# Two casts of v set behind the first product's copy, and down projection rows evicted with high priority

## The chip, the cores and the metric

The kernel runs on one core of one Trainium2 chip. Its time is the device time of one launch in microseconds, as the median of several runs. Engines are named as in the profile: PE is TensorE (matmuls; PEld are its weight loads, which overlap them), DVE is VectorE, ACT is ScalarE, POOL is GpSimd and SP is SyncE. An "ACTq" or "SPq" in front of a line is the engine's own queue issuing a DMA.

## What is computed

Attention with a window of 128 keys and a linear bias per head, over 8 batches, 8 heads, 576 positions and 64 columns per head; its output, with the heads side by side, goes through a bilinear feed-forward layer (512 to 1536 to 512). Everything is float32 at the interface.

```python
scores = scale * np.matmul(q, k.transpose(0, 1, 3, 2))
scores = np.where(mask, scores + bias[None], -1000000000.0)
attn = np.exp(scores - np.max(scores, axis=-1, keepdims=True))
attn = attn / (np.sum(attn, axis=-1, keepdims=True) + 1e-09)
x = np.matmul(attn, v)          # heads laid side by side: 4608 x 512
out = (x @ w_a) * (x @ w_b) @ w_out
```

## The kernel before

The float32 operands are split into two float16 parts each (a rounded one and the rest), and every product is three float16 matmuls into PSUM: high by high, high by low, low by high. Scales that are powers of two keep the parts in range.

The work is woven from two streams. One is the feed-forward layer, batch after batch: an up projection (`up`) and a down projection (`down`). The other is the attention of the batches to come, in steps of one pair of heads (`attention`, four pairs to a batch). A `Pace` object lets the attention advance by a given share at each step of the projections, so that PE always has dense matmuls of the one beside the small ones of the other. During `down` of batch b the attention works through pairs 0 and 1 of the batch after next, and the step that comes with the first step of the next `up` is that for pair 2.

From batch 3 on (and for half of batch 2) the up projection is `up_fast`, a scheme with seven products in place of eight for each of twelve blocks of 128 hidden columns, in steps of six matmuls of 128 x 288. For one block: the first product goes into the PSUM bank `ch`, and ACT copies it to `x0` (line 801). The second goes into another bank, and DVE adds it to `x0` (line 807). The third is *added into* `ch` (so PE may only begin it once the copy of line 801 has read the bank), and ACT scales it into `mid` (line 812, the name `row` in the profile). The fourth is copied by ACT on line 818. The fifth is added into `ch` again, after line 812 has read it, and so on. Blocks run in two lanes: the first four products of the first block come alone, then two of the second lane, then two of the first.

`down` adds 36 matmuls into a bank `dn_ps` for each of eight pieces of the output. ACT scales each piece out of PSUM into one of two `row` buffers (line 875) and issues its store to memory from its own queue (line 876). A store waits for its row, and what stands behind it on ACT waits with it.

A pair's v is split by `split_v`: ACT casts it to float16 (line 277, 128 x 640, the name `vhl`), DVE subtracts to get the rest (line 278). The matmuls of `pv` (line 473, `x_ps`) read both. In the step for pair 2 two pairs are split: that of pair 0, which had to wait for the scale `sv` of the new v (`late`), and that of pair 1. For the scores of a pair, DVE adds the bias and takes the row minimum (line 364), ACT takes the exponential (line 365).

From batch 1 on, PE's order is the one in which the code is written (in the first batch SP's is). The order of all other engines' instructions is set by a scheduler when the program is built: it takes the ready instruction with the highest priority by a modelled timeline, code written earlier having the higher priority, and `tc.high_priority(offset=PRIO)` lifts what is written in its block by 2000. The copies and additions of `up_fast` stand in such blocks, the rows of `down` and the casts of v do not. Once built, each engine works through its own list in order.

Of the kernel before, what the change touches and what calls it, by code (L numbers as in the profile page):

```python
# [17 lines left out]
AF = mybir.ActivationFunctionType  # L18
# [10 lines left out]
HT = S // 2  # L29
# [13 lines left out]
PRIO = 2000  # L43
# [3 lines left out]
def attention_then_bilinear_ffn(ctx: ExitStack, tc: tile.TileContext, qT, kT, vP, w_a, w_b, w_out, rel, slopes2, outT):  # L47
    nc = tc.nc
    vec, act, pe, pool, sp = nc.vector, nc.scalar, nc.tensor, nc.gpsimd, nc.sync
# [224 lines left out]
    def split_v(st, p):  # L274

        vhl = work.tile([P, 2, VCOLS], F16, tag="vhl", name="vhl", bufs=2)
        act.activation(vhl[:, 0, :], st.v[:, p, :], AF.Copy, scale=st.sv)
        vec.scalar_tensor_tensor(out=vhl[:, 1, :], in0=st.v[:, p, :], scalar=st.sv, in1=vhl[:, 0, :], op0=ALU.mult, op1=ALU.subtract)
        return vhl
# [17 lines left out]
    def qk_squares(b, p, qk):  # L297
        o = State()
        o.b, o.p, o.qk = b, p, qk
        sums = small.tile([P, 1], F32, tag="qs", name="qs")  # L300
        hi = work.tile([P, 2, S], F16, tag="qkh", name="qkh", bufs=2)
        lo = work.tile([P, 2, S], F16, tag="qkl", name="qkl", bufs=2)
        act.activation(lo.bitcast(BF16), qk, AF.Square, accum_out=sums)

        o.both = small.tile([P, 2], BF16, tag="both", name="both")
        vec.tensor_scalar(out=o.both, in0=halves, scalar1=sums, scalar2=None, op0=ALU.mult)
        o.kh, o.kl = hi, lo
        return o

    def split_qk(o):  # L310

        b, p, qk, hi, lo = o.b, o.p, o.qk, o.kh, o.kl
        tot = ps_at.tile([P, 512], F32, tag="at", name="qtot")
        pe.matmul(tot[:, 0:2], ones16, o.both, start=True, stop=True)
        sc = small.tile([P, 2], F32, tag="sc", name="sc")
        power_scale(sc, tot[:, 0:2], 1.01, 15)
        own = small.tile([P, 3], F32, tag="own", name="own")
        vec.tensor_tensor_reduce(out=own[:, 0:2], in0=sc, in1=halves, scale=1.0, scalar=0.0, op0=ALU.mult, op1=ALU.add, accum_out=own[:, 2:3])
        own = own[:, 2:3]
        act.activation(hi, qk, AF.Copy, scale=own)  # L320
        vec.scalar_tensor_tensor(out=lo.rearrange("p h s -> p (h s)"), in0=qk.rearrange("p h s -> p (h s)"), scalar=own, in1=hi.rearrange("p h s -> p (h s)"), op0=ALU.mult, op1=ALU.subtract)  # L321
        o.sc = sc
# [298 lines left out]
    def attention():  # L621


        n = NPAIR * (B - 1)
        qks = {}

        def load(i):
            if i < n:

                qks[i] = (load_plain_qk if i < NPAIR else load_qk)(1 + i // NPAIR, i % NPAIR)  # L630

        def squares(i):
            if i >= n:
                return None
            qk = qks.pop(i)
            return qk if i < NPAIR else qk_squares(1 + i // NPAIR, i % NPAIR, qk)

        def split(o):
            if o and o.b > 1:
                split_qk(o)  # L640

        def lay_out(o):
            if o:
                before_scores(o, lay_out_qk(o) if o.b > 1 else -8.0)

        load(0)
        st, prev = load_v(1), None
        o = squares(0)
        lay_out(o)
        load(1)  # L650
        yield 0
        for i in range(n + 1):
            b, p = 1 + i // NPAIR, i % NPAIR
            if o:
                scores(o, 0)
            nxt = squares(i + 1)
            if p == 1 and b > 1:
                st = load_v(b)
            if p == 2:
                late.vhl = split_v(st, late.p)  # L660
            yield i + 1 / 7
            if o:
                scores(o, 1)

            if p == 2:
                pv(late.p, st, late, late.vhl)
                transpose_probs(prev)
            elif prev and p != 1:
                prev.vhl = split_v(st, prev.p)
            yield i + 2 / 7  # L670
            if p == 2:
                split(nxt)
            if o and p != 2:
                normalize(o)
            if p != 2:
                split(nxt)
            yield i + 3 / 7
            if o:
                scores(o, 2)
            if p == 2:  # L680
                prev.vhl = split_v(st, prev.p)
            elif prev and p != 1:
                pv(prev.p, st, prev, prev.vhl)
            yield i + 4 / 7
            if o and p == 2:
                normalize(o)
            if o:
                scores(o, 3)
            lay_out(nxt)
            load(i + 2)  # L690
            if p == 1:
                v_squares(st, (0, 1))
            if prev and p == 0:
                states[b - 1] = st
                assert started["down"] == b - 2
                for k, _ in enumerate(split_x(st, b - 1 <= 2, b - 1 >= 2)):
                    yield i + (4.2 + 0.2 * k) / 7
            yield i + 5 / 7
            if p == 2:
                pv(prev.p, st, prev, prev.vhl)  # L700
            if o:
                normalize(o)
            if p == 1:
                v_squares(st, (2, 3))
            yield i + 6 / 7
            if prev and p == 0:
                hidden_scale(st)
            if p == 1:
                v_scale(st)
                late = prev  # L710
            elif o:
                transpose_probs(o)
            prev, o = o, nxt
            yield i + 1

    states, started = {}, {"down": -1}


    def new_hidden():
        return work.tile([P, 2, HT], F32, tag="rc", name="rc", bufs=3)  # L720
# [72 lines left out]
    def up_fast(st, f, h):  # L793

        ch = ps_ch.tile([P, 512], F32, tag="ch", name="ch")[:, 0:HT]
        hid, mid = new_hidden(), row()
        x0, x1 = hid[:, 0, :], hid[:, 1, :]

        terms(ch, (f, 0), 0, True, True)
        with tc.high_priority(offset=PRIO):  # L800
            act.copy(x0, ch)  # L801
        yield

        ps = ps_ef.tile([P, 512], F32, tag="ef", name="p2")[:, 0:HT]
        terms(ps, (f, 1), 1, True, True)
        with tc.high_priority(offset=PRIO):
            vec.tensor_tensor(out=x0, in0=ps, in1=x0, op=ALU.add)  # L807
        yield

        terms(ch, (f, 4), 5, False, True)  # L810
        with tc.high_priority(offset=PRIO):
            act.activation(mid, ch, AF.Copy, scale=st.g)  # L812
        yield

        ps = ps_ef.tile([P, 512], F32, tag="ef", name="p7")[:, 0:HT]
        terms(ps, (f, 5), 6, True, True)
        with tc.high_priority(offset=PRIO):
            act.copy(x1, ps)  # L818
        yield

        terms(ch, (f, 3), 4, False, True)
        with tc.high_priority(offset=PRIO):
            vec.tensor_tensor(out=x1, in0=ch, in1=x1, op=ALU.add)
        yield

        terms(ps, (f, 2), 3, False, True)
        with tc.high_priority(offset=PRIO):
            vec.scalar_tensor_tensor(out=mid, in0=ps, scalar=st.g, in1=mid, op0=ALU.mult, op1=ALU.add)  # L828
        with tc.high_priority(offset=PRIO):
            pool.tensor_tensor(out=x0, in0=x0, in1=mid, op=ALU.mult)  # L830
        yield

        terms(ch, (f, 6), 2, False, True)
        with tc.high_priority(offset=PRIO):
            vec.scalar_tensor_tensor(out=x1, in0=x1, scalar=st.g, in1=ch, op0=ALU.mult, op1=ALU.mult)  # L835
        with tc.high_priority(offset=PRIO):
            halve(hid, f, h, vec)
        yield
# [25 lines left out]
    def down(b, oi, h, order):  # L864
        started["down"] = b
        for t in range(2):
            for e in range(NE):
                ps = bank("dn_ps")
                for m, f in enumerate(order):
                    for n, (wi, hi) in enumerate(((0, 0), (0, 1), (1, 0))):  # L870
                        pe.matmul(ps[:, 0:HT], wdn[:, f, wi, e * P:(e + 1) * P], h[:, f, t, hi, :], start=(m == 0 and n == 0), stop=(m == NF - 1 and n == 2))  # L871
                    if m % 2 and m < NF - 1:
                        yield
                o = row()
                act.activation(o, ps[:, 0:HT], AF.Copy, scale=oi)  # L875
                act.dma_start(outT[e * P:(e + 1) * P, b * S + t * HT:b * S + (t + 1) * HT], o)
                yield

# [123 lines left out]
```

## Time and profile before

| what | value |
|---|---|
| median of 3 runs | 1061.12 us (1059.61, 1061.12, 1067.57) |
| the profiled execution, its own time | 1065.21 us |
| its span, from first to last instruction | 1063.4 us |
| mean granted TensorE clock | 0.973 |
| busy share of PE, DVE, ACT, POOL | 93%, 66%, 61%, 28% |
| ch of `up_fast`, 1584 matmuls of 128 x 288 | 231.1 us busy, 288 ns each |
| copy of the first product, line 801, 66 times | 26.3 us busy, 399 ns each |
| row of the down projection, line 875, 56 times | 27.6 us busy, 492 ns each |
| cast of v, line 277, 28 times | 22.4 us busy, 822 ns each |

How to read it: the busy time of an engine says how much work it has, not whether it was waited for. That is told by the idle time in brackets in the timeline, and by the table of waits, which names for each wait the engine and line that ended it. The profiled execution is one run; its span is 1.8 us shorter than its own time. The batches from 3 on lie after 500 us, and there are four places at which the up projection of a batch from 3 to 6 begins while the attention is in a step of pair 2: near 500, 617, 735 and 851 us. The up projection of batch 7 has no attention left beside it.

### The profile page before, as it was taken

The page shows a single profiled execution, that of the slowest core. Times are in us where ns is not written, and L with a number is a line of the kernel's source. Part 1 is how long each engine was busy: PE and PEld are TensorE (multiplying, and loading weights), DVE is VectorE, ACT ScalarE, POOL GpSimd, SP SyncE. Part 2 cuts the span into 40 slices and gives each one's busy share as a digit, 9 for nine tenths or more (in the row PEclk, how much of TensorE's full clock was granted, in tenths as well). Part 3 has the DMA queues.
Part 4 walks back from the last instruction along what each step waited for, and adds up shares of the span by engine and source line. Part 5 has one row for each costly group of instructions (what it writes and reads, how often), then busy time and mean ns, then how long its engine had stood idle before and what let it go on. Part 6 is the DMA issues. An engine that isn't in the chain of part 4 may idle for free.

```text
span 1063.4 us, 23921 instructions
## 1 busy us (share of the span) xinstructions
PE 991.9 (93%) x9323; PEld 757.9 (71%) x9323; DVE 697.8 (66%) x1922; ACT 649.3 (61%) x1672; POOL 301.1 (28%) x331
## 2 busy tenths in 40 slices
PE   7678999979999899798999989999999989999998
PEld 5346667757776677575777767777777767777776
DVE  5999976446778646985777657775767576533530
ACT  6786777556767745666656666667656665523321
POOL 3444432100458304871112202230212212220110
PEclk8888999989999899998999999999999999999999
DMA  8344533653623633326423644335514733210000
GB/s 322 125 154 151 190 95 72 127 137 76 125 57 91 163 63 63 84 68 157 86 47 86 170 90 85 61 97 153 114 35 87 177 67 60 40 35 12 2 12 34
DMA packets 148433, 102.83 MB, mean 97 GB/s; under 512 B 120032, under 2 KB 128352, under 8 KB 147296
## 3 DMA queue, kind: packets, MB, share of 16 engines
q1 hardware_dynamic: 134496, 76.04, 31.6%
q10 hardware_dynamic: 13824, 25.27, 6.8%
q8 instruction: 73, 1.20, 0.5%
q14 instruction: 40, 0.33, 0.1%
HBM read 48.33 MB, written 9.44 MB: 54 GB/s over the span
## 4 chain that ended last, share of the span: by engine, by line
PE 46%; DVE 7%; ACT 7%; DMA 6%; issue 2%; SPq 0%; ACTq 0%; DVEq 0%
PE ch L776 15%; PE dn_ps L871 13%; PE p L776 11%; PE up_ps L776 3%; PE x_ps L473 2%; ACT phl L377 2%; DMA qk<-in_kT 2%; DMA v<-in_vP 2%; PE sc_ps L360 2%; DMA pT<-phl 1%; DVE phl L378 1%; DVE qkl L321 1%; ACT t L365 1%; ACT qkh L320 1%; DVE t L364 1%
## 5 line engine op out<-in xcount | busy, mean ns | idle before, releaser
L776 PEld LDWEIGHTS <-wup 128*128 128x128 f16 x4212 | 409.0, 99 | 145.5 <-issue 31.8
L871 PE MATMUL dn_ps<-h,wdn 128*128 128x288 f16 x2016 | 262.5, 289 | 2.3 <-DVE h L770 2.0
L776 PE MATMUL ch<-xs,wup 128*128 128x288 f16 x1584 | 231.1, 288 | 15.1 <-ACT rc L801 6.4
L871 PEld LDWEIGHTS <-wdn 128*128 128x128 f16 x2016 | 194.3, 99 | 58.1 <-issue 2.7
L776 PE MATMUL up_ps<-xs,wup 128*128 128x288 f16 x1440 | 189.1, 292 | 10.9 <-DVE v L590 4.1
L776 PE MATMUL p<-xs,wup 128*128 128x288 f16 x1188 | 178.9, 287 | 1.4 <-ACT rc L818 1.4
L365 ACT ACTIVATE t<-t,mn 128x192 f32<-128x192 f32 (+2 forms) x252 | 107.4, 427 | 73.6 <-DVE mn L364 72.8
L830 POOL TENSOR_TENSOR rc<-rc,row 128x288 f32<-128x288 f32 x66 | 60.1, 910 | 265.5 <-DVE row L828 233.7
L378 DVE SCALAR_TENSOR_TENSOR phl<-t,rin,phl 128x192 f16<-128x192 f32 (+2 forms) x252 | 105.9, 457 | 19.8 <-ACT phl L377 19.2
L377 ACT ACTIVATE phl<-t,rin 128x192 f16<-128x192 f32 (+2 forms) x252 | 88.9, 425 | 22.2 <-DMA pT<-phl 10.8
L769 ACT CAST h<-rc 128x576 f16<-128x576 f32 x96 | 64.0, 667 | 56.0 <-DVE rc L835 29.4
L770 DVE TENSOR_TENSOR h<-rc,h 128x576 f16<-128x576 f32 x90 | 73.0, 811 | 23.9 <-ACT h L769 22.7
L364 DVE CUSTOM_DVE_ANT_0 t<-sc_ps,bias,neg 128x192 f32<-128x192 f32 (+2 forms) x216 | 75.3, 389 | 19.6 <-PE sc_ps L360 19.5
L131 POOL TENSOR_TENSOR wup<-wup,wdn 128x512 int32<-128x512 int32 x36 | 51.9, 1464 | 66.1 <-ACT wdn L126 22.4
L408 DVE TENSOR_TENSOR xs<-v,xs 128x576 f16<-128x576 f32 x51 | 52.3, 1035 | 23.1 <-ACT xs L407 22.8
L807 DVE TENSOR_TENSOR rc<-p,rc 128x288 f32<-128x288 f32 x66 | 30.0, 455 | 52.6 <-PE p L776 50.8
L402 POOL TENSOR_TENSOR xq<-xq,sq 128x576 bf16<-128x576 bf16 x24 | 34.6, 1444 | 87.5 <-ACT sq L401 87.3
L875 ACT ACTIVATE row<-dn_ps,oi 128x288 f32<-128x288 f32 x56 | 27.6, 492 | 51.2 <-PE dn_ps L871 50.5
L812 ACT ACTIVATE row<-ch,g 128x288 f32<-128x288 f32 x66 | 32.6, 494 | 41.7 <-PE ch L776 41.2
L835 DVE SCALAR_TENSOR_TENSOR rc<-rc,g,ch 128x288 f32<-128x288 f32 x66 | 33.6, 509 | 35.1 <-PE ch L776 34.9
L360 PEld LDWEIGHTS <-qst 128*64 128x64 f16 x864 | 30.3, 110 | 32.4 <-issue 31.2
L234 POOL TENSOR_TENSOR wa<-wup 128x512 f32<-128x512 f16 x24 | 33.1, 1381 | 69.2 <-DVE phl L378 62.4
(137 smaller groups left out, 1337.2 us busy)
## 6 DMA issues: line engine op xcount, KB each, us to landing
v<-in_vP SPq DMA_DIRECT2D x8, 1280.0 KB, 6.6
out<-row ACTq DMA_DIRECT2D x64, 144.0 KB, 1.8
qk<-in_qT SPq DMA_DIRECT2D x28, 288.0 KB, 3.9
qk<-in_kT SPq DMA_DIRECT2D x28, 288.0 KB, 4.5
wdn<-in_w_out ACTq DMA_DIRECT2D x12, 512.0 KB, 5.3
wdn<-in_w_a ACTq DMA_DIRECT2D x9, 512.0 KB, 3.9
wdn<-in_w_b ACTq DMA_DIRECT2D x9, 512.0 KB, 4.8
qst<-qkh SPq DMA_DIRECT2D x24, 144.0 KB, 2.6
```

The lines of the kernel that those rows point to most:

```text
L131: pool.tensor_tensor(out=t[:, m, :], in0=t[:, m, :], in1=low[:, m, :], op=ALU.add)
L360: pe.matmul(ps[64 * e:64 * e + 64, c:c + w], o.qs[:, e, qq], ks[:, e, kk], start=not last, stop=last)
L364: vec.tensor_tensor_reduce(out=t[:, c:c + w], in0=ps[:, c:c + w], in1=o.bias[:, WIN - w:WIN], scale=-0.125 if o.b == 1 else o.neg, scalar= ...
L365: act.activation(t[:, c:c + w], t[:, c:c + w], AF.Exp, bias=o.mn[:, n:n + 1], scale=-1.0, accum_out=o.sm[:, n:n + 1])
L377: act.activation(phl[:, 0, pc:pc + w], e, AF.Copy, scale=s)
L378: vec.scalar_tensor_tensor(out=phl[:, 1, pc:pc + w], in0=e, scalar=s, in1=phl[:, 0, pc:pc + w], op0=ALU.mult, op1=ALU.subtract)
L408: vec.tensor_tensor(out=xs[:, n, 1, :, :], in0=src, in1=xs[:, n, 0, :, :], op=ALU.subtract)
L769: act.copy(h[:, f, :, 0, :], hid)
L770: eng.tensor_tensor(out=h[:, f, :, 1, :], in0=hid, in1=h[:, f, :, 0, :], op=ALU.subtract)
L776: pe.matmul(ps[:, 0:HT], wup[:, a[0], a[1], wi, k, :], xs[:, b, xi, k, :], start=(first and n == 0), stop=(last and n == len(ks) - 1), ski ...
L830: pool.tensor_tensor(out=x0, in0=x0, in1=mid, op=ALU.mult)
L871: pe.matmul(ps[:, 0:HT], wdn[:, f, wi, e * P:(e + 1) * P], h[:, f, t, hi, :], start=(m == 0 and n == 0), stop=(m == NF - 1 and n == 2))
```

## The change

```diff
@@ attention
             if p == 2:
-                late.vhl = split_v(st, late.p)
+
+                with tc.issue_after(first_reads[0].ins) if first_reads[0] else ExitStack():
+                    late.vhl = split_v(st, late.p)
...
-    states, started = {}, {"down": -1}
+    states, started, first_reads = {}, {"down": -1}, [None]
@@ up_fast
         with tc.high_priority(offset=PRIO):
-            act.copy(x0, ch)
+            first_reads[:] = first_reads[1:] + [act.copy(x0, ch)]
@@ down
                 o = row()
-                act.activation(o, ps[:, 0:HT], AF.Copy, scale=oi)
+                with tc.high_priority(offset=PRIO):
+                    act.activation(o, ps[:, 0:HT], AF.Copy, scale=oi)
```

`tc.issue_after` ties the instructions of its block that run on ACT, here the cast of the late pair's v, behind the named one in ACT's list; it adds no semaphore. `first_reads` holds the copy of line 801 that was written last. When the code for pair 2 is written, that is the copy of the first block of the up projection that just begins. For the earlier batches, whose up projection begins with the plain scheme, it holds nothing and the cast stays free. The second edit lifts the priority of the rows of `down` when the scheduler chooses.

In the built program the first edit moves instructions at four places, ahead of the up projections of batches 3 to 6, on ACT and DVE only; the four read alike but for buffer numbers. The second moves none: with it alone all five lists are those of before.

ACT's list at the first place, before. `row_6667` and `row_6734` are the last two rows of the down projection, `ch_6737` is the first product's bank, `vhl_6773` the late pair's v, `vhl_7012` that of pair 1:

```order
L875 ACTIVATE row_6667<-dn_ps_6594,oi_6029 128x288
L303 ACTIVATE qkl_6769,qs_6767<-qk_6635 128x1152
L876 DMA out_0<-row_6667 128x288
L277 ACTIVATE vhl_6773<-v_6466,sv_6710 128x640
L277 ACTIVATE vhl_7012<-v_6466,sv_6710 128x640
L875 ACTIVATE row_6734<-dn_ps_6684,oi_6029 128x288
L876 DMA out_0<-row_6734 128x288
L801 COPY rc_6738<-ch_6737 128x288
L365 ACTIVATE t_6748,sm_6633<-t_6748,mn_6632 128x64
```

The same stretch of ACT's list now (lines from 660 on carry numbers higher by 2, from 875 on by 3):

```order
L878 ACTIVATE row_6667<-dn_ps_6594,oi_6029 128x288
L303 ACTIVATE qkl_6769,qs_6767<-qk_6635 128x1152
L879 DMA out_0<-row_6667 128x288
L878 ACTIVATE row_6734<-dn_ps_6684,oi_6029 128x288
L879 DMA out_0<-row_6734 128x288
L803 COPY rc_6738<-ch_6737 128x288
L277 ACTIVATE vhl_6773<-v_6466,sv_6710 128x640
L277 ACTIVATE vhl_7012<-v_6466,sv_6710 128x640
L365 ACTIVATE t_6748,sm_6633<-t_6748,mn_6632 128x64
```

Both casts have gone behind the last row, its store and the copy; the second one was not named, and follows the first.

DVE's list at the same place, before (ISA is the score reduction with its read of the minimum, `p_6776` the second product, the last line the other lane's):

```order
L278 SCALAR_TENSOR_TENSOR vhl<-v,sv,vhl 128x640 x2
L364 ISA t,mn<-sc_ps,bias,neg 128x64
L364 ISA mn 128x1
L364 ISA t,mn<-sc_ps,bias,neg 128x128
L364 ISA mn 128x1
L364 ISA t,mn<-sc_ps,bias,neg 128x192
L364 ISA mn 128x1
L807 TENSOR_TENSOR rc<-p_6776,rc 128x288
L807 TENSOR_TENSOR rc<-p_6809,rc 128x288
```

And now:

```order
L364 ISA t,mn<-sc_ps,bias,neg 128x64
L364 ISA mn 128x1
L364 ISA t,mn<-sc_ps,bias,neg 128x128
L364 ISA mn 128x1
L364 ISA t,mn<-sc_ps,bias,neg 128x192
L364 ISA mn 128x1
L809 TENSOR_TENSOR rc<-p_6776,rc 128x288
L278 SCALAR_TENSOR_TENSOR vhl<-v,sv,vhl 128x640 x2
L809 TENSOR_TENSOR rc<-p_6809,rc 128x288
```

The two subtractions have gone behind the three reductions and the first lane's addition.

## The prediction

> **What bounds the kernel now.** First the page, for the engines' shares; then the second half of the span, because the changed order stands only there; then what TensorE (PE) waits for in that half; last the timeline at the four places where those waits lie.
>
> The page's first lines, then two stretches of the table of windows (length, busy time with count for PE, PEld, DVE, ACT, POOL, then granted clock, DMA share and GB/s):
>
> ```profile
> span 1063.4 us, 23921 instructions
> PE 991.9 (93%) x9323; PEld 757.9 (71%) x9323; DVE 697.8 (66%) x1922; ACT 649.3 (61%) x1672; POOL 301.1 (28%) x331
> ...
> 500.00:1063.40 563.40, 547.55 (x5171) 426.22 (x5168) 333.36 (x940) 313.46 (x814) 104.58 (x101) 1.00 0.33 74
> 621.80:624.00 2.20, 2.20 (x10) 1.41 (x10) 0.90 (x5) 1.72 (x7) 0.00 (x0) 0.50 0.22 72
> ```
>
> From 500 us on PE is busy 547.55 of 563.40 us, 97%, while ACT is busy 313.46. PE is the bound there, and time taken out of a PE wait comes off the end. The second row shows one stretch at half clock, used below.
>
> What PE waits for from 500 us to the end (total, times, longest):
>
> ```profile
> PE ch L776 <- ACT rc L801: 5.9, 4, 2.4
> PE ch L776 <- ACT row L812: 3.2, 4, 0.8
> PE sc_ps L360 <- DMA qkh<-qkh: 1.2, 1, 1.2
> ```
>
> The largest wait, four times, is for ACT's copy on line 801, the first product of an up projection: the very copy the change names. The timeline at the first of the four (start, duration, instruction, in brackets the idle time before it and its releaser):
>
> ```profile
> 501.26 0.19 ACT L303 ACTIVATION_READ_ACCUMULATOR qkl<-qk 128x1 f32 x1
> ...
> 501.79 1.55 ACT L277 ACTIVATE vhl<-v,sv 128x640 f16<-128x640 f32 x2 [0.35 <-DVE sv L110]
> ...
> 502.13 0.91 PE L776 MATMUL p<-xs,wup 128*128 128x288 f16 x6
> 502.65 1.68 DVE L278 SCALAR_TENSOR_TENSOR vhl<-v,sv,vhl 128x640 f16<-128x640 f32 x2 [0.90 <-ACT vhl L277]
> 503.24 0.48 ACT L875 ACTIVATE row<-dn_ps,oi 128x288 f32<-128x288 f32 x1
> ...
> 504.14 0.40 ACT L801 COPY rc<-ch 128x288 f32<-128x288 f32 x1 [0.41 <-ACT row L875]
> ...
> 504.57 0.35 ACT L365 ACTIVATE t<-t,mn 128x64 f32<-128x64 f32 x1
> 504.59 0.90 PE L776 MATMUL ch<-xs,wup 128*128 128x288 f16 x6 [1.54 <-ACT rc L801]
> ...
> 505.74 0.48 ACT L812 ACTIVATE row<-ch,g 128x288 f32<-128x288 f32 x1
> ...
> 507.52 0.90 PE L776 MATMUL ch<-xs,wup 128*128 128x288 f16 x6
> ...
> 508.70 1.63 PE L473 MATMUL x_ps<-pT,vhl 128*64 128x128 f16 x42
> 509.38 0.45 ACT L365 ACTIVATE t<-t,mn 128x192 f32<-128x192 f32 x1 [1.99 <-DVE mn L364]
> ```
>
> ACT casts v twice (1.55 us), evicts the down projection's last row, issues its store, and only then copies ch. PE may not add its next group into ch before that copy, so it stands from 503.04 to 504.59. Nothing needs the casts yet: their first reader on PE is x_ps at 508.70.
>
> **The change part by part.** *The priority of the row evictions: 0.* With that edit alone the program's order is word for word that of before on all five engines, so it has no instruction to move. Both ends of its cost are 0.
>
> *The wait behind the copy.* No instruction is added or removed. At four places, ahead of the up projections of batches 3 to 6, two casts on ACT go from before the row, its store and the copy to behind them; on DVE their two subtractions go behind three score reductions (L364) and one addition (L807). POOL, SP and PE keep their order. The stores are issued from ACT's own queue, so they move up with their rows. Queued behind the casts now: the exponentials (L365), then line 812, whose read of ch holds up PE's third group into ch.
>
> I rebuild ACT's line with the old durations. A row's end to the copy's start, with the store between, is 0.42 us (503.24 + 0.48 to 504.14); a copy's end to PE's start is 0.05 (504.54 to 504.59). from the exponentials' start to the end of line 812 is 505.74 + 0.48 - 504.57 = 1.65. From the second group into ch to the third is 507.52 - 504.59 = 2.93, and in it PE takes four groups of six, one every 0.73.
>
> Place 1. ACT is free at 501.45, whatever the casts do. Row 501.48 to 501.96, copy 502.38 to 502.78, PE allowed at 502.83; its own pace, 502.13 + 0.73, gives 502.86. That is 1.73 earlier than 504.59. Then the casts run 502.81 to 504.36, and the exponentials start at 504.39 instead of 504.57, only 0.18 earlier. So line 812 ends at 506.04, and PE's third group starts at 506.09 where its own pace would give 505.79: a wait of 0.30 comes back. Kept: 507.52 - 506.09 = 1.43.
>
> Place 2:
>
> ```profile
> 618.46 0.34 ACTq L876 DMA_DIRECT2D out<-row  x1
> 618.49 0.91 PE L776 MATMUL p<-xs,wup 128*128 128x288 f16 x6
> 618.98 1.55 ACT L277 ACTIVATE vhl<-v,sv 128x640 f16<-128x640 f32 x2 [0.55 <-DVE sv L110]
> ...
> 621.32 0.40 ACT L801 COPY rc<-ch 128x288 f32<-128x288 f32 x1 [0.41 <-ACT row L875]
> 621.77 1.60 PE L776 MATMUL ch<-xs,wup 128*128 128x288 f16 x6 [2.37 <-ACT rc L801]
> ...
> 626.08 0.90 PE L776 MATMUL ch<-xs,wup 128*128 128x288 f16 x6
> ```
>
> The row needs no sv, so the 0.55 us wait ahead of it goes too: row 618.84 to 619.32, copy 619.74 to 620.14, PE at 620.19, a wait of 0.8 instead of 2.37. The casts end at 621.72, where the copy ended before, so the exponentials start as before at 621.75, line 812 ends at 623.40, and the third group starts at 623.45 instead of 626.08: 2.63. Of these, 626.08 - 621.77 - 2.93 = 1.38 is clock: after the wait of 2.37 the granted clock was 0.50 (the window above), and that group of six lasted 1.60 instead of 0.90. After the waits of 1.54 and 1.50 at places 1 and 3 it lasted 0.90, so I take a wait of 0.8 as free of it.
>
> [...]
>
> Places 3 and 4:
>
> ```profile
> 735.68 0.34 ACTq L876 DMA_DIRECT2D out<-row  x1
> 736.59 0.91 PE L776 MATMUL p<-xs,wup 128*128 128x288 f16 x6
> 738.54 0.40 ACT L801 COPY rc<-ch 128x288 f32<-128x288 f32 x1 [0.41 <-ACT row L875]
> 739.00 0.90 PE L776 MATMUL ch<-xs,wup 128*128 128x288 f16 x6 [1.50 <-ACT rc L801]
> 741.93 0.90 PE L776 MATMUL ch<-xs,wup 128*128 128x288 f16 x6
> ...
> 852.21 0.34 ACTq L876 DMA_DIRECT2D out<-row  x1
> 854.12 0.91 PE L776 MATMUL p<-xs,wup 128*128 128x288 f16 x6
> 855.07 0.40 ACT L801 COPY rc<-ch 128x288 f32<-128x288 f32 x1 [0.41 <-PE p L776]
> 855.51 0.90 PE L776 MATMUL ch<-xs,wup 128*128 128x288 f16 x6 [0.48 <-ACT rc L801]
> ```
>
> Place 3: row 736.06 to 736.54, copy 736.96 to 737.36, PE at 737.41, 1.59 earlier; the casts end at 738.94, line 812 at 740.62, so the third group starts at 740.67 instead of 741.93: 1.26. Place 4: PE reaches this point late, since the scores there wait for a DMA (the 1.2 us above). The copy ends at 853.89, before PE needs it, and PE goes on at 854.85: 0.66, and line 812 is early enough.
>
> Sum: 1.43 + 2.63 + 1.26 + 0.66 = 5.98, say 6.0 us. It lasts if ACT, which is then hardly earlier while PE is, catches up: at 509.38 it sits idle for 1.99 us for scores that PE delivers, more than the 1.4 it has to gain. Next in line is the wait on line 812 (3.2 us in four), which stays: its inputs come from PE as well.
>
> The subtractions. At place 1 the first cast ends at 503.63, its subtraction about 0.85 later at 504.5, the second at 505.3; x_ps comes at 508.70 - 1.43 = 507.27. Cost 0, hidden by 2 us of matmuls. If that cover were gone, x_ps would wait by what is lacking. Bounds of the whole step: at best the four waits whole (5.9), the restart after each (0.91 - 0.73 = 0.18, 0.7 together) and the clock (1.4), 8.0; at worst a loss, in the second rival.
>
> **The rivals.** *Given back 20 us on.* The waits on line 812 (0.8 each) grow by what was won, because ACT and not PE sets the pace through the first exponentials. For it: ACT's line behind the casts moves by only 0.18 us in my sum. Against it: the idle 1.99 us. Only the clock's 1.38 would remain: 1059.7.
>
> *Slower, through the casts.* x_ps would have to wait for the late pair's v. That takes subtractions more than 2 us later than worked out, for instance if DVE sits long at L807, which now stands ahead of them and waits for p and for the copy. It decides once the delay passes that margin by the 1.4 us won. Were DVE to lose 5 us at each place, 4 x (5 - 2) - 6.0 = 6 us would be lost: 1067. Against it: p ends at 503.04 and the copy at 502.78 at place 1, so L807 has both by the time the reductions are through.
>
> *The clock does not come back.* If half rate at place 2 hangs on something other than that wait, 1.38 stays away: gain 4.6, time 1056.5. [...]
>
> *The change does nothing.* For the priority it is so; the casts do move, so it stands only for that half.
>
> **How the numbers follow.** The profiled execution took 1065.21 us around a span of 1063.4; 6.0 less is 1059.2. The median of the runs shown is 1061.12 (1059.61 to 1067.57), 4.1 below the profiled one, and 6.0 less is 1055.1; I say 1055. Chances: as forecast (gain 4.7 to 8) 0.60; no clock won (about 4.6) 0.14; given back (0 to 2) 0.20; slower 0.06. The best case, 8.0, ends at 1053.1; the runs of before lay up to 1.5 below their median, which makes 1051. The given-back case ends at 1061. So 1051 to 1061 leaves out the slower case and the far runs of the others. Within 1% of 1061.12 means 1050.5 to 1071.7, about what a measurement of this kernel tells from no change: nearly everything above lies in it. Faster by over 1% would need 10.6 us, more than all waits named: 0.05. Slower by over 1%: 0.03.
>
> **What would show it.** In the profile of the changed kernel PE's wait on the copy of line 801 falls from 5.9 us in four to under 1.5, the largest at place 2 near 0.8; no stretch at clock 0.50 stands behind place 2; the wait on line 812 gains short entries of about 0.3 at places 1 and 3; no x_ps wait on vhl appears; from the first group into ch at place 1 to that at place 4 the span shrinks by 5.3. Wrong it would be if the waits on line 812 some 20 us behind each place grew past 0.8, or if a place still waited over 1.5.

## The result and the profile after

The changed kernel took 1056.21 us (median of 7 runs, 1054.47 to 1058.28), the kernel before beside it 1062.61 us (7 runs, 1059.61 to 1067.57). The ratio is 0.9929, 95% interval 0.9908 to 0.9951, which is 7.5 us (5.2 to 9.8); the two medians as they stand differ by 6.4 us. The forecast was 1055 with 1051 to 1061, and a change of less than 1% the likeliest; both hold. The profiled execution took 1055.15 us around a span of 1053.4.

The table of PE's waits in the changed kernel from 500 us to the end (total, times, longest), which answers to the one of before. Lines 801 and 812 of before are 803 and 814 now:

```profile
PE ch L778 <- ACT row L814: 3.2, 4, 0.8
PE ch L778 <- ACT rc L803: 1.4, 3, 0.9
PE p L778 <- ACT rc L820: 0.9, 4, 0.2
PE vtot L267 <- DVE vc L264: 0.7, 1, 0.7
PE sc_ps L360 <- DMA qkl<-qkl: 0.3, 1, 0.3
```

The wait on the copy went from 5.9 us in four to 1.4 in three. The next in line kept its size to the tenth (3.2 us in four). No wait on vhl came in.

ACT and PE at the second place in the changed kernel, from the timeline:

```profile
613.06 0.90 PE L778 MATMUL ch<-xs,wup 128*128 128x288 f16 x6
613.82 0.48 ACT L878 ACTIVATE row<-dn_ps,oi 128x288 f32<-128x288 f32 x1
...
614.33 0.34 ACTq L879 DMA_DIRECT2D out<-row  x1
614.36 0.91 PE L778 MATMUL p<-xs,wup 128*128 128x288 f16 x6
614.77 0.50 ACT L878 ACTIVATE row<-dn_ps,oi 128x288 f32<-128x288 f32 x1 [0.47 <-PE sc_ps L360]
615.30 0.34 ACTq L879 DMA_DIRECT2D out<-row  x1
615.68 0.40 ACT L803 COPY rc<-ch 128x288 f32<-128x288 f32 x1 [0.41 <-ACT row L878]
615.98 1.55 ACT L277 ACTIVATE vhl<-v,sv 128x640 f16<-128x640 f32 x2
616.13 0.90 PE L778 MATMUL ch<-xs,wup 128*128 128x288 f16 x6 [0.86 <-ACT rc L803]
...
617.42 0.34 ACT L365 ACTIVATE t<-t,mn 128x64 f32<-128x64 f32 x1
...
618.58 0.48 ACT L814 ACTIVATE row<-ch,g 128x288 f32<-128x288 f32 x1
...
619.11 0.90 PE L778 MATMUL ch<-xs,wup 128*128 128x288 f16 x6
```

Row, store, copy, then the casts: PE waits 0.86 us instead of 2.37, and its group into ch lasts 0.90 instead of 1.60. The row does not start right behind the other row: ACT stands idle for 0.47 us, in which the other row's store is issued (0.34).

Where the 10.0 us between the two spans went can be read from two marks at each place, PE's first and third group into ch. The marks of the changed kernel at places 1, 3 and 4:

```profile
497.36 0.90 PE L778 MATMUL ch<-xs,wup 128*128 128x288 f16 x6
...
503.36 0.90 PE L778 MATMUL ch<-xs,wup 128*128 128x288 f16 x6
...
727.96 0.90 PE L778 MATMUL ch<-xs,wup 128*128 128x288 f16 x6
...
733.62 0.90 PE L778 MATMUL ch<-xs,wup 128*128 128x288 f16 x6
...
842.43 0.90 PE L778 MATMUL ch<-xs,wup 128*128 128x288 f16 x6
...
848.41 0.90 PE L778 MATMUL ch<-xs,wup 128*128 128x288 f16 x6
```

And the first marks of before, whose third ones are 507.52, 626.08, 741.93 and 858.45:

```profile
500.07 1.65 PE L776 MATMUL ch<-xs,wup 128*128 128x288 f16 x6
...
617.20 0.90 PE L776 MATMUL ch<-xs,wup 128*128 128x288 f16 x6
...
734.93 0.90 PE L776 MATMUL ch<-xs,wup 128*128 128x288 f16 x6
...
850.94 0.90 PE L776 MATMUL ch<-xs,wup 128*128 128x288 f16 x6
...
858.45 0.90 PE L776 MATMUL ch<-xs,wup 128*128 128x288 f16 x6
```

| stretch | before, us | after, us | won |
|---|---|---|---|
| start to place 1 (same order in both) | 500.07 | 497.36 | 2.71 |
| place 1, first to third group | 7.45 | 6.00 | 1.45 |
| to place 2 | 109.68 | 109.70 | -0.02 |
| place 2 | 8.88 | 6.05 | 2.83 |
| to place 3 | 108.85 | 108.85 | 0.00 |
| place 3 | 7.00 | 5.66 | 1.34 |
| to place 4 | 109.01 | 108.81 | 0.20 |
| place 4 | 7.51 | 5.98 | 1.53 |
| to the end of the span | 204.95 | 204.99 | -0.04 |

The four places won 7.15 us, and nothing was given back between them. The 2.71 us ahead of place 1 are a difference between two executions of the same order, no part of the change.

Not all of the 7.15 is a shorter wait for the copy, though. At place 4 the scores waited for their DMA in both executions, 1.21 and 0.42 us before:

```profile
853.05 0.22 PE L360 MATMUL sc_ps<-qkh,qst 128*64 128x64 f16 x2 [1.21 <-DMA qkh<-qkh]
853.69 0.22 PE L360 MATMUL sc_ps<-qkl,qst 128*64 128x64 f16 x2 [0.42 <-DMA qkl<-qkl]
```

and 0.26 us in the changed kernel:

```profile
843.74 0.22 PE L360 MATMUL sc_ps<-qkl,qst 128*64 128x64 f16 x2 [0.26 <-DMA qkl<-qkl]
```

So 1.37 of the 1.53 us at place 4 is a shorter DMA wait. The experiments come back to it. At place 1 before's first group ran at half clock (1.65 us, granted clock 0.50 from 500.0 to 501.7 us) while the changed kernel waited 0.58 us for the scores' DMA; to the second product both took about as long (2.06 and 2.13 us).

### The profile page after: what moved, and what is told of

It reads as the page before. It is cut to its first block, busy times and chain, and to the rows that moved or that the text cites. A ratio compares the mean times of both kernels' runs of the same rounds, so it can differ in the third digit from the quotient of the medians.

```text
span 1053.4 us, 23925 instructions
## 1 busy us (share of the span) xinstructions
PE 988.7 (94%) x9323; PEld 756.6 (72%) x9323; DVE 697.8 (66%) x1922; ACT 647.7 (61%) x1672; POOL 299.6 (28%) x331
## 4 chain that ended last, share of the span: by engine, by line
PE 48%; ACT 7%; DVE 6%; DMA 6%; issue 2%; ACTq 0%; SPq 0%; DVEq 0%
PE ch L778 15%; PE dn_ps L873 14%; PE p L778 11%; PE up_ps L778 3%; DMA v<-in_vP 3%; ACT phl L377 2%; PE x_ps L473 2%; PE sc_ps L360 2%; DMA qk<-in_kT 2%; DVE qkl L321 1%; ACT t L365 1%; DVE phl L378 1%; ACT qkh L320 1%; ACT vsq L260 1%; DVE t L364 1%
## 5 line engine op out<-in xcount | busy, mean ns | idle before, releaser
L778 PE MATMUL up_ps<-xs,wup 128*128 128x288 f16 x1440 | 186.6, 289 | 10.3 <-DVE pT L566 3.6
```

What stands on the lines that cost most here:

```text
L778: pe.matmul(ps[:, 0:HT], wup[:, a[0], a[1], wi, k, :], xs[:, b, xi, k, :], start=(first and n == 0), stop=(last and n == len(ks) - 1), ski ...
```

## The experiments

Each is the kernel before or the changed one with the edit shown. Ratios are to the kernel before in the same session. "Way" is the time from the first to the third group into ch, at places 1 to 4.

**The second edit alone.**

```diff
-                act.activation(o, ps[:, 0:HT], AF.Copy, scale=oi)
+                with tc.high_priority(offset=PRIO):
+                    act.activation(o, ps[:, 0:HT], AF.Copy, scale=oi)
```

> Only the second edit, the high priority of the down projection's rows. Theory (it moves no instruction): ratio 1.000 within 0.3%, and PE's wait on the copy of the first product stays at 5.9 us in four from 500 us on, about 1.5, 2.4, 1.5 and 0.5. Rival (the priority brings a part of the gain): 1 to 3 us faster, with shorter waits on that copy. What this run differs by is also the measure of how far two runs of one program differ.

Ratio 0.9993 (0.9977 to 1.0008). The wait in its table:

```profile
PE ch L778 <- ACT rc L803: 6.3, 4, 2.4
```

The priority brings nothing. This is also a second execution of before's program, and its ways are 10.18, 9.18, 7.65 and 7.19 us: place 1 differs from before's 7.45 by 2.7 without any edit, and the timeline tells why:

```profile
501.12 0.22 PE L360 MATMUL sc_ps<-qkh,qst 128*64 128x64 f16 x2 [0.76 <-DMA qkh<-qkh]
501.77 0.26 PE L360 MATMUL sc_ps<-qkl,qst 128*64 128x64 f16 x2 [0.43 <-DMA qkl<-qkl]
...
502.51 1.62 PE L778 MATMUL p<-xs,wup 128*128 128x288 f16 x6
504.92 1.60 PE L778 MATMUL ch<-xs,wup 128*128 128x288 f16 x6 [0.79 <-ACT rc L803]
```

Here the scores waited for their DMA (0.76 and 0.43 us), and the groups behind ran at half clock (granted clock 0.50 from 502 to 508 us).

**The first edit alone.** The rest of the change, with the rows as before.

> Only the first edit, the late cast behind the copy. Theory: the whole gain, 6 to 7.5 us, waits on the copy at most 0.9 us each and 1.4 together. From the first group into ch to the third group into ch it takes about 6.0 us at place 2 (8.88 before, 6.05 with the whole change). At place 4, where the whole change won 1.53 instead of the 0.66 worked out, the sum holds if the scores' wait for their DMA there comes back (over 1 us, as before), and the DMA moved with the change if it stays at 0.3. Rival (the priority does a part): less than 5 us.

Ratio 0.9929 (0.9910 to 0.9947): the whole gain. Ways 5.88, 6.05, 5.55 and 6.05. At place 4 the scores waited 0.41 us for a DMA, not the 1.63 of before. By the sign named above the DMA moved with the change, but the other runs do not bear that out. With the casts where they were at place 4, the wait was 0.26 in the second edit's run, whose program is that of before, and 1.81, 1.39 and 1.66 in the runs below with place 2 alone, one cast more and the filled wait. With the casts moved it was 0.41 or less in this run and both of the whole change, and 2.16 in the last run of all. Long and short waits come with either order. SP issues the DMA only once an earlier transfer (line 329) has landed, and it waited 4.1 us for that in before's profile and 3.0 in the changed one. Over 1 us were four of five executions with the old order and two of eight with the casts moved, so whether the change makes the long wait rarer stays open.

**The first edit at place 2 alone.**

```diff
-                with tc.issue_after(first_reads[0].ins) if first_reads[0] else ExitStack():
+                with tc.issue_after(first_reads[0].ins) if first_reads[0] and b == 5 else ExitStack():
```

> The first edit at place 2 alone, ahead of the up projection of batch 4. Theory (each place gains for itself, and the 2.37 us wait costs a stretch at half clock besides): place 2 takes 6.05 us from the first group into ch to the third instead of 8.88, every group of six there lasts 0.90, places 1, 3 and 4 stay near 7.0 to 7.5, and the time falls by 2.8 us to about 1059.8. Rival (the gain is given back on the way to the next place): the distance from place 2's third group to place 3's first grows by 1 us or more, and the time stays at 1062.6.

Ratio 0.9969 (0.9955 to 0.9983), 3.3 us. Way 2 took 6.05 us, way 3 7.34 and way 4 7.50; from place 2's third group to place 3's first 108.84, as in both kernels. The gain of a place stays where it is made. Way 1 was 10.49, half clock behind DMA waits of 0.96 and 0.42, much as in the second edit's run.

**One cast more.** The kernel before, the copy held behind the store so that the rest keeps its order.

```diff
-        act.activation(vhl[:, 0, :], st.v[:, p, :], AF.Copy, scale=st.sv)
+        for _ in range(2 if twice else 1):
+            act.activation(vhl[:, 0, :], st.v[:, p, :], AF.Copy, scale=st.sv)
...
-                late.vhl = split_v(st, late.p)
+                late.vhl = split_v(st, late.p, 3 < b < 8)
...
-        with tc.high_priority(offset=PRIO):
+        with tc.high_priority(offset=PRIO), tc.issue_after(stores[0].ins) if stores else ExitStack():
             act.copy(x0, ch)
```

> The kernel before with one more cast of v (the late pair's, written twice over) at each of the four places, ahead of the last row, its store and the copy, and all else in its order. Theory (PE waits for whatever ACT does ahead of the copy, and a wait of some 2.3 us costs a stretch at half clock): waits on the copy of about 2.2, 3.1, 2.2 and 1.2, groups of six of about 1.6 instead of 0.90 behind the first three, and the time is 3 us of casts and 1 to 3 us of clock longer: 1066 to 1069. [...] Rival (given back later): no more than 1 us longer, the casts being swallowed by what ACT had to wait for anyway.

Ratio 1.0068 (1.0052 to 1.0085), 7 us slower, a little past the forecast. The second group into ch at the four places:

```profile
504.28 1.48 PE L777 MATMUL ch<-xs,wup 128*128 128x288 f16 x6 [2.68 <-ACT rc L802]
...
623.72 1.46 PE L777 MATMUL ch<-xs,wup 128*128 128x288 f16 x6 [3.09 <-ACT rc L802]
...
742.14 0.90 PE L777 MATMUL ch<-xs,wup 128*128 128x288 f16 x6 [2.40 <-ACT rc L802]
...
743.83 1.65 PE L777 MATMUL ch<-xs,wup 128*128 128x288 f16 x6
...
861.08 0.90 PE L777 MATMUL ch<-xs,wup 128*128 128x288 f16 x6 [1.51 <-ACT rc L802]
```

The waits grew by the cast, 6.3 to 9.7 us in all, and at place 3, which had kept its clock in the kernel before, half clock came in (one group late, 743.83). ACT had no slack to swallow the cast.

**The casts behind the row, ahead of the copy.** The late cast is tied to the last row instead of the copy.

```diff
-            first_reads[:] = first_reads[1:] + [act.copy(x0, ch)]
+            act.copy(x0, ch)
...
-                    act.activation(o, ps[:, 0:HT], AF.Copy, scale=oi)
+                    last = act.activation(o, ps[:, 0:HT], AF.Copy, scale=oi)
+                if b > 1:
+                    first_reads[:] = [last]
```

> As the changed kernel, but the late cast is tied behind the last row of the down projection and not behind the copy: row, two casts, store, copy. The row and its PSUM bank come free as early as with the whole change; the copy does not. Theory (PE waits for the copy alone): waits on the copy stay, about 1.0, 1.9, 1.0 and 0.9 us, shorter than before only by the wait for sv and the store's issue that now lie beside the row and the casts; gain over before 2 to 3.5 us of the 7 to 8. Rival (the late row's PSUM bank held PE up): the whole gain, ratio 0.993.

Ratio 0.9955 (0.9940 to 0.9971), 4.8 us, more than the 2 to 3.5 expected and less than the whole. Its wait:

```profile
PE ch L778 <- ACT rc L803: 5.2, 4, 1.8
```

The row comes early here, and PE still waits for the copy: the bank of the row is not the cause. Ways 7.25, 6.91, 6.61 and 6.91. The surplus fits the clock, in this execution at least: the way at place 2 is 1.97 us shorter than before's, and 1.38 of that lies behind the second group into ch, where after a wait of 1.78 us every group lasted 0.90.

**The wait at place 2 filled.** The kernel before, where PE computes the second product three times over at place 2.

```diff
-        terms(ps, (f, 1), 1, True, True)
+        for _ in range(3 if started["down"] == 3 and f == 0 else 1):
+            terms(ps, (f, 1), 1, True, True)
```

> The kernel before; at place 2 alone PE computes the second product three times over into the same bank, which fills 1.47 us of its 2.37 us wait with matmuls and moves nothing else. Theory (the half clock behind that wait comes of PE's idleness): the copy ends when it did, the wait left is about 0.9 us, the group behind it lasts 0.90 instead of 1.60, the way from the first group into ch to the third is 7.5 us instead of 8.9 to 9.2, and the time falls by 1.4 us although PE does more: ratio 0.9987, at the edge of what can be measured, so the trace decides. Rival (half clock there has another cause, as the state of ACT or the down projection's end): 1.60 again and no change.

The trace:

```profile
617.57 2.38 PE L776 MATMUL p<-xs,wup 128*128 128x288 f16 x18
620.14 0.90 PE L776 MATMUL ch<-xs,wup 128*128 128x288 f16 x6 [0.19 <-ACT rc L801]
```

The group lasts 0.90 and the way is 7.00 instead of 8.88: of the 1.88, 1.38 is the clock, and 0.5 is a copy that came earlier in this execution. In the runs it does not show: ratio 1.0005 (0.9991 to 1.0019), where 0.9987 was expected. Nor does the trace decide. Since the copy came early, the wait without the twelve added matmuls would have been about 0.19 + 1.47 = 1.66 us, and the run before this one kept its clock behind 1.78. So this run does not show that the filling kept the clock, and what half clock at place 2 costs in the mean of many runs stays open. That half clock follows on PE standing idle rests on the other runs. One cast more brought it on at place 3, where the wait grew from 1.50 to 2.40 us. And in a later run of the changed kernel it came at place 1 with no wait for the copy at all, behind idle times of 0.54, 0.78 and 0.40 us, the last two for DMA.

**The copy ahead of the last row.** The changed kernel, with the last row and its store written behind the copy. `store` takes a row and issues its store as before; for the last piece it is called only after the copy.

```diff
-                o = row()
-                with tc.high_priority(offset=PRIO):
-                    act.activation(o, ps[:, 0:HT], AF.Copy, scale=oi)
-                act.dma_start(outT[e * P:(e + 1) * P, b * S + t * HT:b * S + (t + 1) * HT], o)
+                out = outT[e * P:(e + 1) * P, b * S + t * HT:b * S + (t + 1) * HT]
+                if t and e == NE - 1 and 1 < b < B - 2:
+                    held.append((ps, out, oi))
+                else:
+                    store(ps, out, oi)
...
             first_reads[:] = first_reads[1:] + [act.copy(x0, ch)]
+        if held:
+            with tc.issue_after(first_reads[0].ins):
+                store(*held.pop())
...
```

> As the changed kernel, with the last row and its store behind the copy as well: copy, row, two casts, exponentials. Theory (line 812's read of the bank, behind the casts and the exponentials, is next in line): the waits on the copy go from 1.1 to 1.4 in total to near 0, but of the third group into ch only 0.2 to 0.3 us a place are won, 1 us in all: ratio to before 0.992. Rival (the copy is still what PE waits for): about 1.4 us won over the changed kernel and no wait on line 812 there.

Ratio 0.9912 (0.9891 to 0.9932), not to be told from the first edit's 0.9929. No wait on the copy is left from 500 us on; its place in the table is taken by line 812 (818 here):

```profile
PE ch L779 <- ACT row L818: 3.5, 5, 0.8
```

Five waits instead of four, the new one 0.27 at place 2. Ways 5.99, 5.46, 5.61 and 6.07: 0.4 us better in sum than with the first edit alone. The jam moved on to the next reader of the bank, as expected. And the whole gain is there with the row behind the copy, which once more rules out the row's bank.

**The scalings behind the products' copies.** The wait of 0.8 us on line 812 lies some 20 us behind each place: seven scalings of probabilities (line 377) stand ahead of it on ACT. They are written a little later here, and tied behind the copy of line 818.

```diff
+            early = []
             if o and p == 2:
-                normalize(o)
+                if p7s:
+                    early, o.parts = o.parts, []
+                else:
+                    normalize(o)
...
             load(i + 2)
+            if early:
+                yield i + 4.4 / 7
+                late_parts, o.parts, o.n = o.parts, early, o.n
+                with tc.issue_after(p7s[0].ins):
+                    normalize(o, len(early))
+                o.parts = late_parts
...
-            act.copy(x1, ps)
+            p7s[:] = [act.copy(x1, ps)]
```

> As the changed kernel, with the first seven probabilities' scalings of pair 2 (line 377) tied behind the second lane's copies of its products, some 20 us behind each place, where PE waits 0.8 us for line 812 four times. Theory (ACT's list and not its load holds PE up there too): that wait goes from 3.2 us in four to under 0.4, and 2 to 3 us are won over the changed kernel: ratio to before 0.990. Rival (the scalings start 1.3 us later, and the transpose behind them and the next pair's work wait for them): the wait turns up at a later instruction, within 1 us of the changed kernel.

Ratio 0.9915 (0.9894 to 0.9936), not to be told from the first edit's 0.9929. The wait on line 812 is gone, and a copy of line 801 (814 here) is waited for instead:

```profile
PE ch L789 <- ACT rc L814: 2.9, 4, 0.9
...
528.70 0.90 PE L789 MATMUL ch<-xs,wup 128*128 128x288 f16 x6 [0.66 <-ACT rc L814]
```

Of the four waits the longest, 0.86 us, is place 2's own; the other three, of 0.66 each, are new. The rival holds: the wait turned up one block later.

**Both of these, twice.**

> Both of these together. Theory: their gains add, 3 to 4 us over the changed kernel, ratio to before 0.989. Rival: no more than the scalings alone.

> The changed kernel again, beside the next one: ratio to before 0.993, waits on the copy 1.1 to 1.4 us in total.

> Copy before the last row, and the scalings of pair 2 behind the second lane's copies, again, beside the changed kernel on one chip. Theory: 2 to 3 us faster than the changed kernel, ratio to before 0.990. Rival: the two differ by less than 1 us, and the difference seen was one between chips.

The first time 0.9903 (0.9883 to 0.9923); the second, beside the changed kernel, 0.9899 (0.9854 to 0.9944) against 0.9922 (0.9895 to 0.9948), medians 1057.27 and 1057.87 us. Both beat the kernel before; whether the combination beats the changed kernel stays open, since the intervals cover each other.

## Why the prediction was right

*The priority: 0.* Confirmed, 0.9993.

*PE waits for the copy at these places.* Confirmed from four sides: the edit alone brings the whole, one place alone brings its share, one cast more lengthens the wait, an early row without an early copy keeps it at 5.2 us. In before's profile the only other wait of PE there is for the scores' DMA.

*The sum, place by place.* Worked out 1.43, 2.63, 1.26 and 0.66; the two profiled executions differ by 1.45, 2.83, 1.34 and 1.53. The first three were right within 0.2, in part by luck, since two errors of opposite sign lie in them. PE's second group into ch came 3.01, 3.07 and 2.68 us after the first, where the sum has 2.79, 2.99 and 2.48; and the wait on line 812 that was to take some 0.3 us back took 0.05. The fourth term was mis-sized: it rested on PE coming late to that point because the scores waited 1.21 and 0.42 us for their DMA. That wait comes and goes between executions; where it is short the copy is waited for 1.6 us, as the second edit's run shows at its place 4:

```profile
857.86 0.90 PE L778 MATMUL ch<-xs,wup 128*128 128x288 f16 x6 [1.60 <-ACT rc L803]
```

Against its way of 7.19 the changed kernel's 5.98 is a gain of 1.21. Place 1's term, too, was taken from one execution: before's profile shows no half clock behind the copy there, and the three other executions with the old order and no cast more do (ways of 10.18, 10.49 and 10.16). The ways sum to 30.84 and 34.20 us in the two executions of before's program, and to 23.69, 23.53 and 26.24 in the three of the changed one (that of the first edit alone among them); the means differ by 8.0, the runs by 7.5. From so few executions the 8.0 is rough.

*The wait that comes back on line 812.* Worked out as 0.3, found 0.05: at place 2 line 814 ended at 619.06 and PE went on at 619.11, where its pace from 616.13 would have given 619.06. The casts began 0.1 us before the copy ended and the exponentials 0.1 us before the casts ended, where the sum puts each 0.03 behind.

*It lasts.* Confirmed to 0.2 us a stretch by the table of marks; the rival that gives it back is out. So is the slower one: x_ps never waited for vhl.

*The clock.* At place 2 it was won as said in these executions: the group behind the copy lasted 0.90 us instead of 1.60, and the granted clock was 1.00 from 612 to 620 us. The rival in which the clock does not come back gave a gain of 4.6, below the interval. As the sum was low elsewhere too, that alone does not decide; the traces do. Every copy wait of 2.37 us and more in the traces told of here (2.37 in both executions of before's program, 2.40, 2.68, 3.09) was followed by half clock; those of 1.78 and less were not, unless DMA waits lay just ahead. How soon it set in was not the same each time: behind the same 2.37 us the next group ran at half clock in before's profile (1.60), while in the second edit's run it was still at full clock and half clock came with the group after:

```profile
623.68 0.90 PE L778 MATMUL ch<-xs,wup 128*128 128x288 f16 x6 [2.37 <-ACT rc L803]
624.41 1.40 PE L778 MATMUL p<-xs,wup 128*128 128x288 f16 x6
```

Place 1 of the changed program ran at half clock in one execution and not in two others, but there the DMA waits differed as well (0.78 and 0.40 us against 0.19 and 0.39, and 0.46). This is the second group into ch of the one at half clock, the run of the changed kernel beside the combination:

```profile
501.38 1.65 PE L778 MATMUL ch<-xs,wup 128*128 128x288 f16 x6
```

## What to carry to other kernels

An engine that is 56% busy can still hold up one that is 97% busy, as ACT did PE here from 500 us on, through the order of its list: look for the wait that the bound engine has, go to the instruction that ended it, and read what stood ahead of it and when that was needed. Work that is needed 4 us later belongs behind the read that frees the accumulating bank, and one order edge did that here (ratio 0.9929) where a priority moved nothing (0.9993). Before a term is sized from one trace, ask whether the wait beside it belongs to the program or to that execution, since a DMA wait that comes and goes can hide a wait of the program: at place 4 of before's program 1.63 us for DMA went with 0.48 for the copy in one execution, 0.26 with 1.60 in the other.

## What the runs showed of the hardware

Where a store's issue (0.34 us) lay between two instructions of ACT, ACT stood idle around it even if the second did not need the store: 0.47 us between a row and the next one at place 2 of the changed kernel, and 0.42 from a row's end to the copy's start in the kernel before (503.72 to 504.14). It cost nothing where another instruction started ahead of the store: in the changed kernel a row ran from 608.43 to 608.91, an exponential began at 608.82, the store was issued at 608.95 beside it, and the next exponential began at 609.26, where the first ended.

The same program on the same data differed between executions by up to 2.7 us within one stretch of 10 us (7.45 and 10.18 at place 1), when DMA waits of 0.43 and 0.76 us were followed by half clock on PE. Such waits do not always lead to it: 1.39 us for a DMA and then 1.51 for the copy, at place 4 with one cast more, did not.
